# Weight conversion wholly through PSUM, block sums ranked last, and a last batch in two equal parts

## The chip, the cores and the metric

The kernel runs on one core of one Trainium2 chip. The metric is the device time of one execution in microseconds (us), as the median of several runs. One further execution is recorded by the hardware profiler; its rows are what this text reads.

## What is computed

```python
# B, H, S, D = 4, 8, 768, 64
k_sum = k.reshape(B, H, 24, 32, D).max(axis=3)
v_sum = v.reshape(B, H, 24, 32, D).mean(axis=3)
scores_l = where(|pos_q - pos_k| < 16, scale * q @ k.T, -1e9)
scores_s = scale * q @ k_sum.T + log(32)
a = softmax(concat([scores_l, scores_s]))
x = a @ concat([v, v_sum])            # -> [B, S, 512]
...
h = relu(x.T @ w_tok1) @ w_tok2       # 768 -> 256 -> 768 over tokens
u = x + h.T
out = u + relu(u @ w_ch1) @ w_ch2     # 512 -> 1536 -> 512 over channels
```

All in float32. The weights are doubles in memory and reach the core as such.

## The kernel before

**Stages.** Each batch goes through attention (local window of 96 keys and 24 block summaries for each tile of 64 queries, heads in four pairs p), the token mix (`t1`, then `up`), and the channel mix. The channel mix takes most of the time. It is done in two halves of the tokens, 512 and 256 (`HT`), and in 12 slices f of the inner 1536: `ch1` puts u @ w_ch1 of one slice in a PSUM tile `hp` (12 matmuls), ACT writes its relu rounded (L843) and DVE the remainder (L848) into `h`, and `ch2` adds h @ w_ch2 to four output tiles `acc` (12 matmuls, L874). A float32 product is three passes with a rounded part and a remainder of each operand (`w1h`, `w1l`, `w2h`, `w2l`). In a name such as hp_0_0_8 the numbers are batch, half and slice; in sc_8_0 and et_8_0, and in av_8, the first is batch times 8 plus head.

**What runs beside it.** While PE works through the channel mix of batch b, the attention of batch b+1 is put between the products: scores `sc` (24 matmuls), softmax on DVE and ACT (`e`, L440 and L450), transposes `et`, and `av`. For batch 1 this stands in the last slices of batch 0 and later. The softmax output x is put away to memory in the transposed layout (`xaway`) and fetched again as `xT` (`fetch_x`, L530), where DVE adds the token mix to it (L787) and ACT and POOL split the sum into u. The block sums of v are loaded separately (`vb`, L268), reduced by DVE into `vs` (L382, eight of 96x512 for batch 1), scaled by POOL (L390) and written behind v by a DMA (v<-vs, L295); `av` reads them.

**The weights** are converted on the chip, in 30 ticks of 128x512 values. Ticks 6 to 29 are the channel weights: tick 6+2f is w1 of slice f, tick 7+2f is w2 of it. A tick is a load of the 64-bit words (L1005, SP queue), |high word| on ACT (L1035), a clamp on POOL (L1039), three steps on DVE (shift L1044, sign L1051, low bits L1058), the rounded part on ACT (L1080) and the remainder on POOL (L1086). What the shift and the sign leave is kept in `between`:

```python
psum = 10 <= i < 24
...
if psum:
    pb = bank(f"wp_{i}", ["att"])
    between, bkey = (lambda: pb.t.bitcast(I32)), (pb, 0)
else:
    between, bkey = mid, parts[0]
```

so ticks 10 to 23 keep it in a PSUM bank of the tag `att` (two banks, which the attention's scores use too; name `wp`), the others in SBUF (name `wb`). Ticks run during batch 0's first half, a few slices ahead of their use.

**The order.** A planner (class `Plan`) simulates the engines with a cost for each step (`took`), gives each step a rank (`R_H`, `R_EVAC`, `R_ATT`, `R_LATER`, `R_W`, from 0 to 4, the lowest first) and writes out one fixed order for each engine. An engine then takes its instructions in that order and waits at the first that isn't ready. SP issues nearly all DMAs, in one queue.

Of the kernel before, what the change touches and what calls it, by code (L numbers as in the profile page):

```python
# [34 lines left out]
HT = (512, 256)  # L35
H0 = (0, 512)
# [150 lines left out]
def tile_attention_mixer(  # L187
# [438 lines left out]
    def turn_x(b, p):  # L626

        x2, a = x_t[b, p]
        e = sbuf([P, S], "e", f"xb_{b}_{p}", 3)
        add(  # L630
            "dve", 1.05,
            lambda: nc.vector.transpose(
                e.t.rearrange("p (t c) -> p t c", c=P), x2.t[:, :, a, :]
            ),
            reads=x_keys(b, p), writes=[(e, 0)], rank=R_ATT,
        )
        for half, nt in enumerate(HT):
            cs = slice(H0[half], H0[half] + nt)
            away = xa_t[b, half, p] = plan.slot(
                dram, [P, nt], F32, f"xaway{half}", f"xaway_{b}_{half}_{p}", 4  # L640
            )
            add(
                "sp", 0.4, lambda away=away, cs=cs: nc.sync.dma_start(out=away.t, in_=e.t[:, cs]),
                reads=[(e, 0)], writes=[(away, 0)], kb=nt // 2,
            )
# [103 lines left out]
    def tok2(b, half, p):  # L749
        (x2, a), t1 = x_t[b, p], t1_t[b, p]  # L750
        h0, nt = H0[half], HT[half]
# [4 lines left out]
        u = u_t[b, half, p] = sbuf([P, 2, nt], f"u{half}", f"u_{b}_{half}_{p}", 4, F32R)  # L756
# [25 lines left out]
        if far:  # L782
# [3 lines left out]
                "dve", 0.6 if half == 0 else 0.42,  # L786
# [6 lines left out]
                "act", 0.5 if half == 0 else 0.38,  # L793
# [13 lines left out]
            "act", 0.5 if half == 0 else 0.38,  # L807
# [4 lines left out]
            "dve", 0.6 if half == 0 else 0.42,  # L812
# [8 lines left out]
    def ch1(b, half, f):  # L821
        nt = HT[half]
        pt = mm_bank(f"hp_{b}_{half}_{f}")
        h = h_t[f] = sbuf([P, 2, nt], ("h", "ot")[half], f"h_{b}_{half}_{f}", 2, F32R)
# [3 lines left out]
        def products():  # L828
# [13 lines left out]
            "act", 0.5 if half == 0 else 0.36,  # L842
# [4 lines left out]
            "dve", 0.57 if half == 0 else 0.37,  # L847
# [10 lines left out]
    def ch2(b, half, f):  # L858
        h, nt = h_t.pop(f), HT[half]
# [128 lines left out]
    def w_tick(i, behind=()):  # L988
# [22 lines left out]
        psum = 10 <= i < 24  # L1011
# [57 lines left out]
        add("dve", 0.6 if psum else 0.5, shift, reads=parts, writes=[bkey], rank=rank)  # L1069
# [62 lines left out]
    start = [sum(HT[j // NF] // 256 for j in range(i)) for i in range(2 * NF + 1)]  # L1132
    for b in range(B):
# [126 lines left out]
```

## Time and profile before

| | us |
|---|---|
| median of three runs | 582.44 (581.02 to 582.76) |
| the profiled execution, device time | 582.82 |
| its span, first to last instruction | 581.0 |
| TensorE matmul (PE) busy | 564.6 (97%) |
| VectorE (DVE) busy | 288.3 (50%) |
| ScalarE (ACT) busy | 216.6 (37%) |
| GpSimd (POOL) busy | 153.5 (26%) |

An idle stretch of PE is where time can be had, as long as PE's work stays what it is. The time of an idle stretch is read from the rows in which PE waits, and what it waited for stands in brackets behind it.

### The profile page before, as it was taken

The numbers are of one execution on the slowest core, as the hardware profiler recorded it, in microseconds if no ns is written. First come the engines' busy times: TensorE is split into PE (matmuls) and PEld (weight loads), VectorE is DVE, ScalarE is ACT, GpSimd is POOL, SyncE is SP. The second block draws the span as 40 slices with busy tenths as digits, with TensorE's granted clock in tenths as the row PEclk, the third lists the DMA queues.
The fourth block names the chain that finished last, engine by engine and source line by source line (L and its number), as shares of the span: only waits on it lengthen the run. The fifth ranks groups of instructions, "written<-read, shape, count | busy, mean of one in ns | idle before, by whom it ended". The sixth has DMA issues, their size and how long they took to land.

```text
span 581.0 us, 12315 instructions
## 1 busy us (share of the span) xinstructions
PE 564.6 (97%) x4701; PEld 487.9 (84%) x4701; DVE 288.3 (50%) x872; ACT 216.6 (37%) x697; POOL 153.5 (26%) x191
## 2 busy tenths in 40 slices
PE   7889999989999999999999999999999998999997
PEld 3678888768989988878899988888899997888997
DVE  3698799996563255644733336442543321110311
ACT  4677665536564343222334224222434111110110
POOL 0236586744033310000085010000085021000500
PEclk9999999989999999999999999999999999999999
DMA  8854568643664027847775127745454012000101
GB/s 294 304 164 129 184 211 263 215 154 129 193 193 152 18 74 198 231 109 200 213 177 131 23 56 190 199 134 136 123 142 91 6 26 49 1 0 1 70 4 37
DMA packets 116778, 75.89 MB, mean 131 GB/s; under 512 B 86640, under 2 KB 99056, under 8 KB 116720
## 3 DMA queue, kind: packets, MB, share of 16 engines
q1 hardware_dynamic: 116720, 75.12, 45.8%
q8 instruction: 37, 0.61, 0.4%
q14 instruction: 21, 0.17, 0.1%
HBM read 57.59 MB, written 15.73 MB: 126 GB/s over the span
## 4 chain that ended last, share of the span: by engine, by line
PE 80%; DVE 11%; DMA 4%; ACT 2%; issue 2%; SPq 1%; POOL 1%; DVEq 0%; ACTq 0%
PE acc L874 30%; PE hp L831 29%; PE t1q L730 5%; PE up L770 4%; PE av L557 4%; PE sc L426 4%; DMA w<-in_w_ch 2%; DVE wb L1058 2%; PE warm L1099 1%; PE et L488 1%; DMA k<-in_kw 1%; DVE wb L1051 1%; DVE wp L1051 1%; DVE wp L1044 1%; DVE vs L382 1%
## 5 line engine op out<-in xcount | busy, mean ns | idle before, releaser
L874 PE MATMUL acc<-h,w2h 128*128 128x512 f32 (+1 forms) x768 | 205.0, 340 | 2.1 <-DVE h L848 2.1
L831 PE MATMUL hp<-u,w1h 128*128 128x512 f32 (+1 forms) x768 | 191.5, 339 | 0.0
L874 PEld LDWEIGHTS acc<-h,w2h 128*128 128x128 f32 x768 | 134.4, 189 | 20.6 <-DVE h L848 3.3
L831 PEld LDWEIGHTS hp<-u,w1h 128*128 128x128 f32 x768 | 131.2, 190 | 16.2 <-issue 1.3
L848 DVE SCALAR_TENSOR_TENSOR h<-hp,h 128x512 fp32r<-128x512 f32 (+1 forms) x96 | 53.2, 554 | 161.1 <-ACT h L843 161.0
L831 PE MATMUL hp<-u,w1l 128*128 128x256 f32 (+1 forms) x384 | 129.4, 337 | 0.3 <-POOL w1l L1086 0.3
L874 PE MATMUL acc<-h,w2l 128*128 128x256 f32 (+1 forms) x384 | 129.2, 336 | 0.0
L843 ACT ACTIVATE h<-hp 128x512 fp32r<-128x512 f32 (+1 forms) x96 | 46.9, 488 | 205.4 <-PE hp L831 204.3
L450 ACT ACTIVATE e<-e,den 128x120 f32<-128x120 f32 x192 | 73.3, 385 | 49.8 <-DVE den L440 49.7
L831 PEld LDWEIGHTS hp<-u,w1l 128*128 128x128 f32 x384 | 72.6, 189 | 8.4 <-POOL w1l L1086 0.7
L874 PEld LDWEIGHTS acc<-h,w2l 128*128 128x128 f32 x384 | 72.5, 189 | 6.9
L935 POOL TENSOR_TENSOR ot<-ot,u 128x512 f32<-128x512 f32 (+1 forms) x28 | 29.1, 1062 | 133.0 <-DVE ot L927 133.0
L440 DVE CUSTOM_DVE_ANT_0 e<-sc,mask_sb 128x120 f32<-128x120 f32 x192 | 41.4, 277 | 13.7 <-PE sc L426 12.4
L770 PE MATMUL up<-wt2h,t 128*128 128x256 f32 (+1 forms) x128 | 37.3, 350 | 1.6 <-DVE xT L787 1.6
L409 POOL MEMSET e<- 128x48 f32 x16 | 2.3, 141 | 131.1 <-DMA away<-e 68.6
L450 ACT ACTIVATION_READ_ACCUMULATOR e<-e,den 128x1 f32 x192 | 36.2, 189 | 0.0
L716 POOL TENSOR_TENSOR xs<-x,xs 128x512 fp32r<-128x512 f32 x18 | 23.5, 1306 | 28.1 <-ACT xs L711 28.1
L426 PE MATMUL sc<-k,q 64*64 64x120 f32 x768 | 28.6, 274 | 1.8 <-PE et L488 0.7
L426 PEld LDWEIGHTS sc<-k,q 64*64 64x64 f32 x768 | 20.9, 134 | 10.7 <-issue 6.8
L730 PE MATMUL t1q<-xs,ws 128*128 128x256 f32 x216 | 28.7, 284 | 0.0
L557 PEld LDWEIGHTS av<-v,eT 120*64 120x64 f32 x768 | 23.9, 138 | 4.8 <-issue 2.5
L730 PEld LDWEIGHTS t1q<-xs,ws 128*128 128x128 f32 x216 | 27.2, 191 | 0.4
(73 smaller groups left out, 595.0 us busy)
## 6 DMA issues: line engine op xcount, KB each, us to landing
w<-in_w_ch SPq DMA_DIRECT2D x48, 256.0 KB
k<-in_kw SPq DMA_DIRECT2D x16, 720.0 KB
v<-in_vw SPq DMA_DIRECT2D x32, 288.0 KB
q<-in_q SPq DMA_DIRECT2D x16, 384.0 KB
away<-e SPq DMA_DIRECT2D x16, 384.0 KB
eT<-away SPq DMA_DIRECT2D x64, 96.0 KB
out<-ot SPq DMA_DIRECT2D x16, 256.0 KB
w<-in_w_tok SPq DMA_DIRECT2D x12, 256.0 KB
```

The costliest lines, as they stand in the source:

```text
L426: nc.tensor.matmul(tiles[j].t[c * QT : (c + 1) * QT, i * NC : (i + 1) * NC], lhsT=qt.t[rows, t * QT : (t + 1) * QT], rhs=kt.t[rows, t, :], ...
L440: nc.vector.tensor_tensor_reduce(out=e.t[:, j, i * P : i * P + NC], in0=tiles[j].t[:, i * NC : (i + 1) * NC], in1=mask_sb[:, mv, :], op0=A ...
L450: nc.scalar.activation(ei, ei, AF.Exp, bias=den_t[n].t[:, 1, T : T + 1], scale=-1.0, accum_out=den_t[n].t[:, 0, T : T + 1],)
L557: nc.tensor.matmul(pv[cs, T], lhsT=eT[:NC, T % (TT // 2), cs], rhs=v.t[:NC, 2 * T + c], start=True, stop=True,)
L716: lambda slot=slot, src=src: nc.gpsimd.tensor_tensor(out=slot.t[:, 1], in0=src(), in1=slot.t[:, 0].bitcast(F32), op=ALU.subtract),
L730: nc.tensor.matmul(pt.t[:, 2 * P * k : 2 * P * (k + 1)], lhsT=ws[:, wp, T, ks], rhs=xs[:, xp, T], start=(c == 0 and k == 0 and T == 0 and ...
L770: nc.tensor.matmul(pt.t[:, :nt], lhsT=t1.t[:, part, ks], rhs=w[:, k, h0 : h0 + nt], start=(far and k == 0 and i == 0), stop=(k == DTOK // ...
L831: nc.tensor.matmul(pt.t[:, :nt], lhsT=w[:, c, fs], rhs=us[c].t[:, part], start=(i == 0), stop=(i == len(ops) - 1),)
L843: lambda: nc.scalar.activation(h.t[:, 0], pt.t[:, :nt], AF.Relu),
L848: lambda: nc.vector.scalar_tensor_tensor(out=h.t[:, 1], in0=pt.t[:, :nt], scalar=0.0, in1=h.t[:, 0].bitcast(F32), op0=ALU.max, op1=ALU.sub ...
L874: nc.tensor.matmul(slot.t[:, c0 : c0 + nt], lhsT=w[:, f, o * P : (o + 1) * P], rhs=h.t[:, part], start=(f == 0 and w is w2h and part == 0 ...
L935: lambda view=view, u=u: nc.gpsimd.tensor_tensor(out=view(), in0=view(), in1=u.t[:, 1].bitcast(F32), op=ALU.add),
```

## The change

1. All channel-weight ticks from 10 on keep `between` in PSUM, so ticks 24 to 29 too. The planner's costs of the DVE steps are set anew.
2. The eight block sums of v for batch 1 get rank `R_W + 1`, behind the weights, instead of `R_LATER`, before them.
3. The last batch is cut 384/384 instead of 512/256, and the planner's costs follow the width (`spent`). The put-away x goes in slots by width; u of its second half takes other tags; its `acc` tiles take a bank each in both halves; the outputs of its first half are kept in tag `k`.
4. `fetch_x` of the second half comes a slot earlier in the program, and the last two odd output DMAs go through ACT's queue.

```diff
-HT = (512, 256)
-H0 = (0, 512)
+HT = ((512, 256),) * (B - 1) + ((384, 384),)
+H0 = ((0, 512),) * (B - 1) + ((0, 384),)
...
-            reads=[(slot, 0)], writes=[(s, ("sum", c))], rank=R_LATER,
+            reads=[(slot, 0)], writes=[(s, ("sum", c))], rank=R_W + 1 if b == 1 else R_LATER,
...
-                dram, [P, nt], F32, f"xaway{half}", f"xaway_{b}_{half}_{p}", 4
+                dram, [P, nt], F32, f"xaway{nt}", f"xaway_{b}_{half}_{p}", 8
...
+    def spent(nt, quarter, half):
+
+        return quarter + (half - quarter) * (nt - 256) / 256
...
-        u = u_t[b, half, p] = sbuf([P, 2, nt], f"u{half}", f"u_{b}_{half}_{p}", 4, F32R)
+        tag, bufs = f"u{half}", 4
+        if b == B - 1 and half:
+            tag, bufs = (("e", 3), ("q", 2))[p // 2]
+        u = u_t[b, half, p] = sbuf([P, 2, nt], tag, f"u_{b}_{half}_{p}", bufs, F32R)
...
-        h = h_t[f] = sbuf([P, 2, nt], ("h", "ot")[half], f"h_{b}_{half}_{f}", 2, F32R)
+        h = h_t[f] = sbuf([P, 2, nt], "ot" if nt == 256 else "h", f"h_{b}_{half}_{f}", 2, F32R)
...
-                    slot = sbuf([P, n, nt], "h", f"ot_{b}_{half}_{o}", 2)
+                    slot = sbuf([P, n, nt], "k" if nt == 384 else "h", f"ot_{b}_{half}_{o}", 2)
...
-            add(
-                "sp", 0.06,
-                lambda view=view, o=o: nc.sync.dma_start(
+            eng, queue = ("act", nc.scalar) if o in ur_t and o % 2 else ("sp", nc.sync)
+            add(
+                eng, 0.06,
+                lambda view=view, o=o, queue=queue: queue.dma_start(
...
-        psum = 10 <= i < 24
+        psum = i >= 10
...
         stt = 0.7 if room else 0.85
+        if not psum and not first:
+            stt = 0.95 if room else 1.2
...
-        add("dve", 0.6 if psum else 0.5, shift, reads=parts, writes=[bkey], rank=rank)
+        add("dve", 0.69, shift, reads=parts, writes=[bkey], rank=rank)
...
+                if b >= FAR and u1s[p] == slot + 1:
+                    fetch_x(b, 1, p)
                 if u1s[p] == slot:
-                    if b >= FAR:
-                        fetch_x(b, 1, p)
                     tok2(b, 1, p)
```

How the order moves is shown at three places. The first is DVE in batch 0, where the weights of slice 9 (ticks 24 and 25) begin. Before, the last block sum stands between ticks 22 and 23, seven others stand further up, and tick 24 works in SBUF:

```order
L1058 SCALAR_TENSOR_TENSOR wb_22_1338<-w_22_1279,wp_22_1461 128x512
L382 TENSOR_REDUCE vs_1_1310<-vb_1_7_1451 96x16
L1044 TENSOR_SCALAR wp_23_1489<-wb_23_1365 128x512
L848 SCALAR_TENSOR_TENSOR h_0_0_7_1481<-hp_0_0_7_1438,h_0_0_7_1481 128x512
L1051 SCALAR_TENSOR_TENSOR wp_23_1489<-w_23_1303,wp_23_1489 128x512
L1058 SCALAR_TENSOR_TENSOR wb_23_1365<-w_23_1303,wp_23_1489 128x512
L1044 TENSOR_SCALAR wb_24_1402<-wb_24_1402 128x512
```

After, the same stretch of DVE's order:

```order
L1067 SCALAR_TENSOR_TENSOR wb_22_1340<-w_22_1279,wp_22_1417 128x512
L1053 TENSOR_SCALAR wp_23_1438<-wb_23_1369 128x512
L1060 SCALAR_TENSOR_TENSOR wp_23_1438<-w_23_1305,wp_23_1438 128x512
L1067 SCALAR_TENSOR_TENSOR wb_23_1369<-w_23_1305,wp_23_1438 128x512
L1053 TENSOR_SCALAR wp_24_1465<-wb_24_1399 128x512
L1060 SCALAR_TENSOR_TENSOR wp_24_1465<-w_24_1333,wp_24_1465 128x512
L1067 SCALAR_TENSOR_TENSOR wb_24_1399<-w_24_1333,wp_24_1465 128x512
L856 SCALAR_TENSOR_TENSOR h_0_0_7_1486<-hp_0_0_7_1440,h_0_0_7_1486 128x512
```

Tick 24 is done before the remainder of slice 7 (h_0_0_7), and no block sum stands there. They now follow the last weight step, among the work of slices 10 and 11; six stand ahead of the first softmax of batch 1 (e_4_0) and two behind it:

```order
L1067 SCALAR_TENSOR_TENSOR wb_29_1518<-w_29_1467,wp_29_1604 128x512
L384 TENSOR_REDUCE vs_1_1629<-vb_1_0_1263 96x16
L384 TENSOR_REDUCE vs_2_1633<-vb_2_0_1514 96x8
L384 TENSOR_REDUCE vs_1_1629<-vb_1_1_1265 96x16
L384 TENSOR_REDUCE vs_1_1629<-vb_1_2_1267 96x16
L856 SCALAR_TENSOR_TENSOR h_0_0_10_1655<-hp_0_0_10_1614,h_0_0_10_1655 128x512
L313 TENSOR_REDUCE ks_5_1676<-k_5_1572 128x24
L322 COPY k_5_1572<-ks_5_1676 128x12x24
L384 TENSOR_REDUCE vs_1_1629<-vb_1_3_1636 96x16
L384 TENSOR_REDUCE vs_2_1633<-vb_2_1_1639 96x8
L384 TENSOR_REDUCE vs_1_1629<-vb_1_4_1659 96x16
L856 SCALAR_TENSOR_TENSOR h_0_0_11_1706<-hp_0_0_11_1679,h_0_0_11_1706 128x512
```

The second place is PE in batch 0 at slice 8. Before, `hp` of slice 8 follows the twelve `acc` products of slice 7 and is followed by `hp` of slice 9:

```order
L874 MATMUL acc_0_0_3_1089<-h_0_0_7_1481,w2h_78 128x512
L831 MATMUL hp_0_0_8_1527<-u_0_0_0_886,w1h_76 128x512 x2
L831 MATMUL hp_0_0_8_1527<-u_0_0_0_886,w1l_77 128x512
L831 MATMUL hp_0_0_8_1527<-u_0_0_1_909,w1h_76 128x512 x2
L831 MATMUL hp_0_0_8_1527<-u_0_0_1_909,w1l_77 128x512
L831 MATMUL hp_0_0_8_1527<-u_0_0_2_934,w1h_76 128x512 x2
L831 MATMUL hp_0_0_8_1527<-u_0_0_2_934,w1l_77 128x512
L831 MATMUL hp_0_0_8_1527<-u_0_0_3_1014,w1h_76 128x512 x2
L831 MATMUL hp_0_0_8_1527<-u_0_0_3_1014,w1l_77 128x512
L831 MATMUL hp_0_0_9_1555<-u_0_0_0_886,w1h_76 128x512 x2
```

After, PE has `hp` of slice 8 ahead of the `acc` products of slice 7:

```order
L882 MATMUL acc_0_0_3_1092<-h_0_0_6_1424,w2h_78 128x512
L839 MATMUL hp_0_0_8_1501<-u_0_0_0_893,w1h_76 128x512 x2
L839 MATMUL hp_0_0_8_1501<-u_0_0_0_893,w1l_77 128x512
L839 MATMUL hp_0_0_8_1501<-u_0_0_1_913,w1h_76 128x512 x2
L839 MATMUL hp_0_0_8_1501<-u_0_0_1_913,w1l_77 128x512
L839 MATMUL hp_0_0_8_1501<-u_0_0_2_937,w1h_76 128x512 x2
L839 MATMUL hp_0_0_8_1501<-u_0_0_2_937,w1l_77 128x512
L839 MATMUL hp_0_0_8_1501<-u_0_0_3_1015,w1h_76 128x512 x2
L839 MATMUL hp_0_0_8_1501<-u_0_0_3_1015,w1l_77 128x512
L882 MATMUL acc_0_0_0_1089<-h_0_0_7_1486,w2h_78 128x512
```

So a product of twelve matmuls now stands between each `hp` and the `acc` that needs it. Behind this, slices 9 to 11 alternate in the same way, and the first scores of batch 1 (sc_8_0, sc_9_0) stand one product earlier.

The third place is PE at the start of the last batch, where the token mix of the second half (`up`, pairs 2 and 3) still has to be done. Before, the two stand in a row ahead of the first `acc`:

```order
L770 MATMUL up_3_1_2_5807<-wt2l_82,t1_3_2_5492 128x256
L770 MATMUL up_3_1_2_5807<-wt2h_81,t1_3_2_5492 128x256
L770 MATMUL up_3_1_3_5819<-wt2h_81,t1_3_3_5495 128x256
L770 MATMUL up_3_1_3_5819<-wt2l_82,t1_3_3_5495 128x256
L770 MATMUL up_3_1_3_5819<-wt2h_81,t1_3_3_5495 128x256 x2
L770 MATMUL up_3_1_3_5819<-wt2l_82,t1_3_3_5495 128x256
L770 MATMUL up_3_1_3_5819<-wt2h_81,t1_3_3_5495 128x256
L874 MATMUL acc_3_0_0_5829<-h_3_0_0_5794,w2h_78 128x512
```

After, the first `acc` product (twelve matmuls, the first three shown) stands between pair 2 and pair 3:

```order
L779 MATMUL up_3_1_2_5807<-wt2l_82,t1_3_2_5514 128x384
L779 MATMUL up_3_1_2_5807<-wt2h_81,t1_3_2_5514 128x384
L882 MATMUL acc_3_0_0_5817<-h_3_0_0_5798,w2h_78 128x384
L882 MATMUL acc_3_0_0_5817<-h_3_0_0_5798,w2l_79 128x384
L882 MATMUL acc_3_0_0_5817<-h_3_0_0_5798,w2h_78 128x384
```

## Rows read from the trace of the kernel before

**Rows 1.** The page, its first part: busy us, share and instructions of each engine.

```profile
PE 564.6 (97%) x4701; PEld 487.9 (84%) x4701; DVE 288.3 (50%) x872; ACT 216.6 (37%) x697; POOL 153.5 (26%) x191
```

**Rows 2.** Windows: stretch, length, busy of PE, PEld, DVE, ACT, POOL, PEclk, DMA, GB/s.

```profile
66.00:106.00 40.00, 40.00 (x178) 32.84 (x177) 36.05 (x65) 24.22 (x57) 28.22 (x42) 1.00 0.74 228
106.00:123.00 17.00, 14.61 (x55) 10.78 (x53) 16.76 (x26) 6.98 (x18) 13.41 (x16) 0.90 0.69 224
```

**Rows 3.** Waits of PE: who waited for whom, us in total, times, longest.

```profile
PE et L488 <- DVE x L569: 0.8, 1, 0.8
```

**Rows 4.** Timeline of PE, 106 to 123: start, us, instruction [idle before <- releaser].

```profile
106.90 0.39 PE L874 MATMUL acc<-h,w2l 128*128 128x512 f32 x1
107.61 0.74 PE L874 MATMUL acc<-h,w2h 128*128 128x512 f32 x2 [0.32 <-DVE h L848]
...
112.77 0.61 PE L831 MATMUL hp<-u,w1h 128*128 128x512 f32 x2
113.66 0.50 PE L831 MATMUL hp<-u,w1l 128*128 128x512 f32 x1 [0.27 <-POOL w1l L1086]
...
116.36 0.39 PE L874 MATMUL acc<-h,w2l 128*128 128x512 f32 x1
118.55 0.73 PE L874 MATMUL acc<-h,w2h 128*128 128x512 f32 x2 [1.80 <-DVE h L848]
...
122.44 0.72 PE L831 MATMUL hp<-u,w1h 128*128 128x512 f32 x2
```

**Rows 5.** Timeline of DVE: two ticks in PSUM form, then the late ones in SBUF.

```profile
75.23 0.69 DVE L1044 TENSOR_SCALAR wp<-wb 128x512 int32<-128x512 int32 x1
...
77.29 0.69 DVE L1044 TENSOR_SCALAR wp<-wb 128x512 int32<-128x512 int32 x1
...
105.69 0.68 DVE L382 TENSOR_REDUCE vs<-vb 96x16 f32<-96x512 f32 x1
...
108.80 0.42 DVE L1044 TENSOR_SCALAR wb<-wb 128x512 int32<-128x512 int32 x1
...
111.02 0.96 DVE L1044 TENSOR_SCALAR wb<-wb 128x512 int32<-128x512 int32 x1
...
114.07 0.97 DVE L1044 TENSOR_SCALAR wb<-wb 128x512 int32<-128x512 int32 x1
```

**Rows 6.** Groups of DVE by form: count | busy us, mean ns | idle before.

```profile
L382 DVE TENSOR_REDUCE vs<-vb 96x16 f32<-96x512 f32 x8 | 5.1, 673 | 0.0
```

**Rows 7.** Timeline of POOL: the same remainder step beside PSUM and SBUF ticks.

```profile
106.83 1.44 POOL L1086 TENSOR_TENSOR w1l<-wb,w1h 128x256 fp32r<-128x256 f32 x2
...
112.42 2.33 POOL L1086 TENSOR_TENSOR w1l<-wb,w1h 128x256 fp32r<-128x256 f32 x2
```

**Rows 8.** Timeline of ACT: the longest wait for a weight's load.

```profile
92.69 0.66 ACT L1035 ACTIVATE wb<-w 128x512 f32<-128x512 f32 x1 [1.82 <-DMA w<-in_w_ch]
```

**Rows 9.** Timeline of PE, later: the first scores of batch 1.

```profile
128.09 0.85 PE L426 MATMUL sc<-k,q 64*64 64x120 f32 x24
```

**Rows 10.** Timeline of DVE at 170: the block maximum ahead of x.

```profile
170.22 0.95 DVE L311 TENSOR_REDUCE ks<-k 128x24 f32<-128x768 f32 x1 [2.10 <-DMA k<-in_kw]
```

**Rows 11.** Timeline of PE and DVE at the start of the last batch.

```profile
473.82 0.63 PE L831 MATMUL hp<-u,w1h 128*128 128x512 f32 x2
...
481.33 0.42 DVE L787 TENSOR_TENSOR xT<-up,xT 128x256 f32<-128x256 f32 x1 [2.62 <-DMA xT<-xaway]
...
481.81 0.39 PE L770 MATMUL up<-wt2h,t 128*128 128x256 f32 x1 [1.64 <-DVE xT L787]
```

**Rows 12.** The chain that ended last: twelve matmuls of 512 and of 256 columns.

```profile
510.00 2.72 PE acc L874 x12
...
569.83 1.45 PE hp L831 x12
```

**Rows 13.** Timeline of DVE and SP at the end.

```profile
576.37 1.46 DVE L927 TENSOR_TENSOR ur<-acc,ur 128x256 f32<-128x256 f32 x4 [1.35 <-PE acc L874]
...
576.82 1.79 SPq L942 DMA_DIRECT2D out<-ur  x4
```

More of the change, by code (lines that the diff above doesn't have):

```diff
@@ L636, in turn_x @@
         )
-        for half, nt in enumerate(HT):
-            cs = slice(H0[half], H0[half] + nt)
+        for half, nt in enumerate(HT[b]):
+            cs = slice(H0[b][half], H0[b][half] + nt)
             away = xa_t[b, half, p] = plan.slot(
-                dram, [P, nt], F32, f"xaway{half}", f"xaway_{b}_{half}_{p}", 4
+                dram, [P, nt], F32, f"xaway{nt}", f"xaway_{b}_{half}_{p}", 8
             )
@@ L774, in products @@
                     )
-        took = (1.45, 0.75) if far else (2.0, 1.1)
         add(
-            "pe", took[half], products,
+            "pe", spent(nt, 0.75, 1.45) if far else spent(nt, 1.1, 2.0), products,
             reads=([] if far else x_keys(b, p)) + [(t1, 0), (t1, 1)] + [("wt2", i) for i in range(3)],
@@ L785, in tok2 @@
             add(
-                "dve", 0.6 if half == 0 else 0.42,
+                "dve", spent(nt, 0.42, 0.6),
                 lambda: nc.vector.tensor_tensor(
@@ L792, in tok2 @@
             add(
-                "act", 0.5 if half == 0 else 0.38,
+                "act", spent(nt, 0.38, 0.5),
                 lambda: nc.scalar.activation(u.t[:, 0], xT.t, AF.Copy),
@@ L806, in tok2 @@
         add(
-            "act", 0.5 if half == 0 else 0.38,
+            "act", spent(nt, 0.38, 0.5),
             lambda: nc.scalar.activation(u.t[:, 0], pt.t[:, :nt], AF.Copy),
@@ L811, in tok2 @@
         add(
-            "dve", 0.6 if half == 0 else 0.42,
+            "dve", spent(nt, 0.42, 0.6),
             lambda: nc.vector.tensor_tensor(
@@ L841, in ch1 @@
         add(
-            "act", 0.5 if half == 0 else 0.36,
+            "act", spent(nt, 0.36, 0.5),
             lambda: nc.scalar.activation(h.t[:, 0], pt.t[:, :nt], AF.Relu),
@@ L846, in ch1 @@
         add(
-            "dve", 0.57 if half == 0 else 0.37,
+            "dve", spent(nt, 0.37, 0.57),
             lambda: nc.vector.scalar_tensor_tensor(
@@ L858, in ch2 @@
     def ch2(b, half, f):
-        h, nt = h_t.pop(f), HT[half]
+        h, nt = h_t.pop(f), HT[b][half]
         n = 512 // nt
@@ L896, in residual @@
     def residual(b, half, o):
-        u = u_t[b, half, o]
-        slot = ur_t[o] = sbuf([P, 2 * HT[0]], "u0", f"ur_{o}", 4)
+        u, nt = u_t[b, half, o], HT[b][half]
+        slot = ur_t[o] = sbuf([P, nt], "u0", f"ur_{o}", 4)
         add(
-            "pool", 0.7,
+            "pool", spent(nt, 0.7, 1.2),
             lambda: nc.gpsimd.tensor_tensor(
-                out=slot.t[:, : HT[half]], in0=u.t[:, 0].bitcast(F32),
+                out=slot.t, in0=u.t[:, 0].bitcast(F32),
                 in1=u.t[:, 1].bitcast(F32), op=ALU.add,
@@ L909, in finish @@
     def finish(b, half):
-        h0, nt = H0[half], HT[half]
-        n = 2 * HT[0] // nt
+        h0, nt = H0[b][half], HT[b][half]
+        n = 1024 // nt
         for o in range(NC4):
             u, (bank_o, c0) = u_t.pop((b, half, o)), acc[o]
-            took = 0.57 if half == 0 else 0.37
+            took = spent(nt, 0.37, 0.57)
             if o in ur_t:
                 slot = ur_t[o]
-                view = lambda slot=slot: slot.t[:, :nt]
+                view = lambda slot=slot: slot.t
                 key, other, more = (slot, 0), view, [(slot, 0)]
@@ L933, in finish @@
                 add(
-                    "pool", 1.2 if half == 0 else 0.7,
+                    "pool", spent(nt, 0.7, 1.2),
                     lambda view=view, u=u: nc.gpsimd.tensor_tensor(
@@ L1128, in tile_attention_mixer @@
     tok2(0, 0, NP - 1)
-    start = [sum(HT[j // NF] // 256 for j in range(i)) for i in range(2 * NF + 1)]
+    start = [sum(HT[0][j // NF] // 256 for j in range(i)) for i in range(2 * NF + 1)]
     for b in range(B):
```

12 lines of the change are left out of this document (6 added, 6 removed).

## The prediction

> **What bounds the kernel now.** I read the page first: PE is busy for 97% of the span [rows 1], so a change can only win where PE stands still, runs slowly, or is left waiting at either end. The windows, the list of PE's waits and its timeline then say where that is. From 66 to 106 PE has no gap, while DVE is busy for 36.05 of 40 us. From 106 to 123 PE is busy for only 14.61 of 17 us at a mean clock of 0.90, and DVE for 16.76 of 17 [rows 2]. That is the stage of the late weights: DVE is what is late, and PE pays. The timeline of PE gives the price [rows 4]. Twelve 512-column matmuls take 2.72 us when nothing disturbs them, 0.227 each [rows 12]. The matmul at 106.90 is followed after 0.71 (0.48 too much, waiting for the remainder of h), the pair at 112.77 after 0.89 (0.44 too much, for POOL's remainder of w1), the one at 116.36 after 2.19 (1.96 too much, for h again). Together 2.9 us. Behind the last one PE needs 3.89 us, from 118.55 to 122.44, for ten matmuls that are worth 2.27: the clock fell to the lower level after the long wait, and that costs another 1.6. So this stage loses **4.5 us**.
>
> Elsewhere there is little: 0.8 where `et` waits for x at about 172 [rows 3], 1.64 at the start of the last batch [rows 11], and the tail, in which the last evacuations start at 576.37 and the last output is issued at about 578.6 [rows 13] while the span ends at 581.0. The sum is made against the profiled execution's own 582.82, which lies 0.38 above the median of 582.44.
>
> **Part 1, the block sums.** Eight reduces of 96x512 cost DVE 5.1 us [rows 6], all before the late weights; the last ends just after 106 [rows 5]. Behind the weights they cost the same, but the first eleven slices no longer wait for them. So tick 24, which DVE begins at 108.80 [rows 5], can begin some 5 us earlier. What could take DVE's place as the late one is the load: the longest wait of ACT for a weight is 1.82 at 92.69 [rows 8]. It eats at most that much of the 5 us, and three block-sum loads of 192 KB also leave the queue's stretch there.
>
> **Part 2, PSUM for ticks 24 to 29.** A tick in PSUM form takes 2.06 (75.23 to 77.29). In SBUF form tick 24 takes 2.22 and tick 25 3.05 [rows 5], the latter while POOL works. POOL suffers too: the same remainder step takes 1.44 beside PSUM ticks and 2.33 beside SBUF ones [rows 7]. I take a gain of 2 us on DVE over the six ticks (bounds: a loss of about 2, when POOL is idle and the shift's 0.69 instead of 0.42 [rows 5] counts in full, and a gain of 6, at 1 us a tick). None of this is on the path by itself: it adds to the 5 us.
>
> The shift shows 0.42 with both sides in SBUF and 0.69 with PSUM. The Trainium skill ("VectorE: DVE Perf Modes", section "Why PSUM operands drop a tier") says that a PSUM operand rules out the mode that needs both SBUF read ports, which speaks against this part: by that page alone the six ticks would cost DVE 6 x 0.27 = 1.6 more. Its page "SBUF — State Buffer", section "Who interferes with whom", says that a DVE instruction with two SBUF inputs contends with a GpSimd one that reads SBUF, and one with a single SBUF input doesn't; that speaks for it, and the slow rows on both engines agree. I count the stretch by the rows.
>
> **Sum of the stage.** With 5 + 2 us in hand, w1 of slice 8 is ready at about 104 instead of 108.3 (the remainder step at 106.83 [rows 7]), so PE can take `hp` of slice 8 at 106.9, right behind `acc` of slice 6, as the order of after has it. Its remainder h would be ready at about 112.3; `acc` of slice 8 comes up at about 106.9 + 3 x 2.72 = 115.1. Before, h was late by 2; now it is early by almost 3. All three waits go, and with them the half-speed stretch, since nothing else stops PE there: **-4.5**. What is late next are the two PSUM banks. The first scores of batch 1 (sc_8_0) come one product earlier and reuse banks that ticks 28 and 29 now hold until about 120.6, while PE gets there at about 120.2: **+0.4** (0 to 1.5). Queued behind that wait on PE are `acc` of slice 9 and all that follows, so every tenth of it counts.
>
> On DVE the block sums now stand among slices 10 and 11 and ahead of the first softmax. Six of them, 4 us, delay e_4_0 to about 129 to 130; the second scores, which need its bank back, come up at about 131: hidden, with under 1 us to spare. v of batch 1 is complete once POOL has scaled vs and the DMA has landed, by my count at about 135; `av` of batch 1 comes at about 144: hidden by 9 us. On SP the block-sum loads moved behind w_29, and k and q of batch 1 with them; the scores of batch 1 stood at 128.09 before [rows 9] and their loads still come first among those moved: nothing.
>
> **Part 3, 384/384.** No row has 384 columns. Twelve matmuls take 2.72 at 512 and 1.45 at 256 [rows 12], so on a straight line 2.09 at 384, and two halves of 384 cost what one of 512 and one of 256 cost: **0**. The far bounds are the rates of the two neighbours, 0.121 and 0.227 a matmul against my 0.173, which over 576 matmuls would be about -30 and +31 us; I take the line between them, since the two rows make a step of 0.015 plus 0.00041 a column, so that nearly all of a matmul is its columns, and keep +-1 us. At the half boundary four `acc` banks must be evacuated instead of reused in pairs, four steps of under 0.69 beside two `hp` products of 2.1 each: hidden.
>
> At the **start of the last batch** PE waits 1.64, 1.92 from start to start less the matmul's own 0.12 = 1.8 in all [rows 11]: `up` of pair 3 needs the bank that DVE frees by adding xT, and xT came late from memory (2.62). In the new order the first `acc` product of 2.1 us lies between pair 2 and pair 3, and the fetch is issued a slot earlier, but `up` of pair 2 comes one wait forward. From the spacing of SP's issues I get waits of about 0.35 and 0.6: **-0.85** (0 to -1.8).
>
> The **tail**: the last `acc` is four groups of three matmuls of 384, with one evacuation of about 0.55 behind the last (0.36 a piece for 256 columns by [rows 13]), and the four output issues (0.45 each on one queue, [rows 13]) go over two queues. Against that, 768 KB instead of 512 KB have to land. **-0.3** (+0.3 to -0.6). Here the Trainium skill ("DMA: Bandwidth & Descriptors", section "Issuing engines are not separate DMA queues") warns that a second issuing engine saves only the issuing time; by it alone the longer transfer would make the tail 0 to +0.3. No row separates the two.
>
> **The rest**: x at 172 waits for ks, which waited 2.10 for its load [rows 10]; a vb load ahead of it has moved, so some 0.6 earlier: **-0.3** (0 to -0.8). In the first 60 us a few steps change places (vm of pair 3 ahead of `av`), for which I see no reason either way: 0 (+-0.8). At the end of batch 0 `up` of pair 3 comes closer to the first `hp` that needs it: **+0.1** (0 to 0.3). Batches 1 and 2 keep PE's order.
>
> Sum: -4.5 + 0.4 - 0.85 - 0.3 - 0.3 + 0.1 = -5.45 against 582.82, so 577.4; on the scale of the median **577.0**.
>
> **The rivals.**
> A, the forecast: the stage of the late weights closes up. 577.0, with its own range of 574.8 to 579.5.
> B, the wait only moves: the banks of ticks 28 and 29, or the six block sums ahead of e_4_0, stop PE at the first or second scores. Margins of +0.4 and under 1 us are thin, and DVE is full until 130. If it happens for about as long as the wait removed, PE also loses its clock again: 577.0 - 0.4 + 1.96 + 1.6 = 580.2.
> C, the change doesn't do what it says: the weights were held back by their loads, not by DVE (the 1.82 in [rows 8] and a DMA share of 0.74 speak for it; DVE's 36.05 of 40 against [rows 2]), so slice 8's weights come no sooner and the 4.5 us stay, now as a wait at the earlier `hp`. Only the rest remains: 582.44 - 0.85 - 0.3 - 0.3 = 581.0.
> D, slower: v of batch 1 is late. The last two block sums stand behind e_4_0's softmax, then come POOL's scaling and a DMA in SP's one queue, behind k and q. `av` of batch 1 needs it at about 144, and each us beyond that is a us of PE. From 147.5 on the gain over the range of equal times is gone, from 151 on the kernel is slower by over 0.3%; a landing at 153 gives 577.0 + 9 = 586. My count of 135 speaks against, the long queue on SP for it.
>
> **How the numbers follow.** A 0.60, B 0.20, C 0.11, D 0.09. The prediction is A's 577.0. A measurement of this kernel tells 0.3%, 1.75 us, from no change: faster is below 580.7, slower above 584.2. A gives all of its chance to faster, B about three quarters; C lies within; D is mostly slower: faster 0.75, same 0.16, slower 0.09. The range of 574.5 to 581.5 takes in A, B and most of C; it leaves out D and about as much in the outer parts of the others.
>
> **What would show it.** Right: between 106 and 123 PE has no wait over 0.3 for h or w1l and its clock stays at the upper level; L1058 of ticks 24 to 29 shows 0.7 and POOL's L1086 about 1.4; `sc` at about 120 waits for under 1 us. B: PE waits for L1058 or L440 between 119 and 133. C: ACT's waits for loads between 90 and 105 grow to over 4 us. D: `av` of batch 1 waits for a DMA. The part on 384 is wrong if a product of twelve takes other than 2.05 to 2.13; the start of the last batch is right if its two waits sum to under 1.2.

## The result

The changed kernel takes 578.18 us (median of 14 runs, 574.71 to 580.4) where the kernel before takes 582.75 (14 runs as well). The ratio is 0.990 (0.9876 to 0.9925), so 4.4 to 7.2 us less. 577.0 (574.5 to 581.5) was forecast.

The profiled execution took 574.71, with a span of 572.9 against 581.0. That pair overstates the difference: its first scores came at 7.28 instead of 8.47, because the warm-up ran at the higher clock earlier (its matmuls start 0.43 us apart until 4.2 us into the span here and until 6.6 in the trace before, and 0.22 apart behind that). That is no work of the change: no_actq, which has the same start, came to them at 8.29 (more on it at the end). I therefore read the difference by stretches that hold the same work in every kernel:

| stretch | before | after | |
|---|---|---|---|
| up to the first scores | 8.47 | 7.28 | -1.19 |
| from there to the first channel product of batch 0 | 57.16 | 57.62 | +0.46 |
| **batch 0**: from there to the first product of batch 1 | 141.70 | 135.09 | **-6.61** |
| batches 1 to 3, to the end of the last matmul | 369.63 | 369.25 | -0.39 |
| tail, to the end of the span | 4.07 | 3.68 | -0.39 |

Batch 0 is read between the first `hp` products of batch 0 and of batch 1, before and then after:

```profile
65.63 0.63 PE L831 MATMUL hp<-u,w1h 128*128 128x512 f32 x2
...
207.33 0.63 PE L831 MATMUL hp<-u,w1h 128*128 128x512 f32 x2
```

```profile
64.90 0.63 PE L839 MATMUL hp<-u,w1h 128*128 128x512 f32 x2
...
199.99 0.63 PE L839 MATMUL hp<-u,w1h 128*128 128x512 f32 x2
```

The page and the windows of the stage, after; the rows of before are [rows 1] and [rows 2], and the columns are the same:

```profile
PE 560.2 (98%) x4701; PEld 497.8 (87%) x4701; DVE 283.0 (49%) x872; ACT 215.6 (38%) x697; POOL 152.4 (27%) x191
```

```profile
66.00:106.00 40.00, 40.00 (x178) 33.10 (x178) 36.06 (x63) 26.28 (x62) 31.11 (x47) 1.00 0.72 225
106.00:123.00 17.00, 17.00 (x96) 13.80 (x95) 16.62 (x32) 5.92 (x14) 9.04 (x13) 1.00 0.62 210
```

PE is busy without a gap from 106 to 123 at the full clock, where it had 14.61 of 17 us at 0.90. DVE is as full as before; it is only further ahead. PE's timeline, where [rows 4] showed three waits, has none; the products of slices 7 to 10 and the first scores follow each other directly:

```profile
105.72 0.61 PE L839 MATMUL hp<-u,w1h 128*128 128x512 f32 x2
...
108.44 0.39 PE L882 MATMUL acc<-h,w2h 128*128 128x512 f32 x1
...
111.17 0.61 PE L839 MATMUL hp<-u,w1h 128*128 128x512 f32 x2
...
113.89 0.39 PE L882 MATMUL acc<-h,w2h 128*128 128x512 f32 x1
...
116.61 0.61 PE L839 MATMUL hp<-u,w1h 128*128 128x512 f32 x2
...
119.42 0.84 PE L428 MATMUL sc<-k,q 64*64 64x120 f32 x23
```

On DVE the remainder of h for slice 7 and the one for slice 8 are there 3 us before `acc` asks for them at 108.44 and 113.89, the copy of k that the first scores need is done at 117.5, and the last weight step at 118.1:

```profile
104.59 0.68 DVE L856 SCALAR_TENSOR_TENSOR h<-hp,h 128x512 fp32r<-128x512 f32 x1
...
110.15 0.68 DVE L856 SCALAR_TENSOR_TENSOR h<-hp,h 128x512 fp32r<-128x512 f32 x1
...
117.16 0.31 DVE L322 COPY k<-ks 128x288 f32<-128x288 f32 x1
117.39 0.68 DVE L1067 SCALAR_TENSOR_TENSOR wb<-w,wp 128x512 int32<-128x512 int32 x1
117.99 2.19 DVE L384 TENSOR_REDUCE vs<-vb 96x16 f32<-96x512 f32 x4
```

### The profile page after: what moved, and what is told of

It is laid out like the page before. It is cut to its first block, busy times and chain, and to the rows that moved or that the text cites. A ratio compares the mean times of both kernels' runs of the same rounds, so it can differ in the third digit from the quotient of the medians.

```text
span 572.9 us, 12330 instructions
## 1 busy us (share of the span) xinstructions
PE 560.2 (98%) x4701; PEld 497.8 (87%) x4701; DVE 283.0 (49%) x872; ACT 215.6 (38%) x697; POOL 152.4 (27%) x191
## 4 chain that ended last, share of the span: by engine, by line
PE 90%; DVE 4%; ACT 3%; POOL 1%; issue 1%; SPq 1%; DMA 0%; DVEq 0%
PE hp L839 35%; PE acc L882 35%; PE t1q L736 5%; PE up L779 5%; PE sc L428 4%; PE av L559 4%; ACT e L452 2%; PE et L490 1%; PE warm L1110 1%; ACT eT L501 1%; PE up L771 1%; PE t1p L689 0%; DVE wb L1060 0%; ACT wb L1044 0%; DMA xT<-xaway 0%
## 5 line engine op out<-in xcount | busy, mean ns | idle before, releaser
L882 PE MATMUL acc<-h,w2h 128*128 128x512 f32 (+2 forms) x768 | 205.8, 338 | 0.0
L839 PE MATMUL hp<-u,w1h 128*128 128x512 f32 (+2 forms) x768 | 192.7, 338 | 0.0
L839 PEld LDWEIGHTS hp<-u,w1h 128*128 128x128 f32 x768 | 132.7, 189 | 12.6 <-issue 1.4
L856 DVE SCALAR_TENSOR_TENSOR h<-hp,h 128x512 fp32r<-128x512 f32 (+2 forms) x96 | 53.0, 552 | 154.5 <-ACT h L851 154.4
L839 PE MATMUL hp<-u,w1l 128*128 128x512 f32 (+2 forms) x384 | 128.9, 336 | 0.0
L882 PE MATMUL acc<-h,w2l 128*128 128x512 f32 (+2 forms) x384 | 128.4, 334 | 0.0
L851 ACT ACTIVATE h<-hp 128x512 fp32r<-128x512 f32 (+2 forms) x96 | 46.9, 489 | 201.5 <-PE hp L839 200.2
L943 POOL TENSOR_TENSOR ot<-ot,u 128x512 f32<-128x512 f32 (+2 forms) x28 | 27.9, 1018 | 108.8 <-DVE ot L935 107.4
L779 PE MATMUL up<-wt2h,t 128*128 128x256 f32 (+2 forms) x128 | 37.7, 352 | 1.1 <-DVE xT L795 0.7
```

The costliest lines, as they stand in the source:

```text
L779: nc.tensor.matmul(pt.t[:, :nt], lhsT=t1.t[:, part, ks], rhs=w[:, k, h0 : h0 + nt], start=(far and k == 0 and i == 0), stop=(k == DTOK // ...
L839: nc.tensor.matmul(pt.t[:, :nt], lhsT=w[:, c, fs], rhs=us[c].t[:, part], start=(i == 0), stop=(i == len(ops) - 1),)
L851: lambda: nc.scalar.activation(h.t[:, 0], pt.t[:, :nt], AF.Relu),
L856: lambda: nc.vector.scalar_tensor_tensor(out=h.t[:, 1], in0=pt.t[:, :nt], scalar=0.0, in1=h.t[:, 0].bitcast(F32), op0=ALU.max, op1=ALU.sub ...
L882: nc.tensor.matmul(slot.t[:, c0 : c0 + nt], lhsT=w[:, f, o * P : (o + 1) * P], rhs=h.t[:, part], start=(f == 0 and w is w2h and part == 0 ...
L943: lambda view=view, u=u: nc.gpsimd.tensor_tensor(out=view(), in0=view(), in1=u.t[:, 1].bitcast(F32), op=ALU.add),
```

## The experiments

All times are medians, with the kernel before run beside them (583.2 to 583.9). "Batch 0" is the stretch of the table above, in the profiled execution. It is the same work in all of these kernels (late_dve adds to it).

**The three edits that touch the weight stage.** They are the rank of the block sums, the PSUM form of ticks 24 to 29, and the planner's costs of the DVE steps. First each was taken out of the changed kernel.

no_rank, the sums ahead of the weights again:

```diff
-rank=R_W + 1 if b == 1 else R_LATER
+rank=R_LATER
```

> The changed kernel, with the block sums of batch 1 ranked ahead of the weights again (5.1 us of DVE). Theory DVE-late (the gain comes from taking those sums out of DVE's way): the wait for h before the acc of slice 8 is back, less what PSUM ticks save, 1 to 3 us in all and the lower clock behind it, so about 581 (580 to 582.5). Theory PSUM (the gain comes from the PSUM form of ticks 24 to 29, the sums were covered anyway): no wait over 0.5, 578 to 579. Theory loads (weights wait for their DMAs): the same wait of PE in this kernel and in the changed one, 578 to 579, with ACT waiting for loads just as long.

Measured: 578.85, ratio 0.9918 (0.9892 to 0.9944); batch 0 137.18. In the weight stage PE waits 0.34 once, at the scores. Most of the gain stays without the rank.

no_psum, ticks 24 to 29 in SBUF:

```diff
-psum = i >= 10
+psum = 10 <= i < 24
```

> The changed kernel, with ticks 24 to 29 in SBUF form again. Theory DVE-late: the sums' 5 us cover the 2 us or so that the SBUF form costs, no wait of PE over 0.5 between 100 and 125, 578 to 579. Theory PSUM: the waits are back, 581 to 583. Either way the steps L1067 of these ticks take 0.9 to 1.1 where POOL works and POOL's remainder 1.8 to 2.3, against 0.7 and 1.4 to 1.6.

Measured: 578.19, ratio 0.9899 (0.9863 to 0.9934); batch 0 135.03. Nothing is lost, though the steps are as slow as foretold: 1.12 for L1067 where POOL works.

Then the rank alone, on the kernel before (only_rank):

```diff
-rank=R_LATER
+rank=R_W + 1 if b == 1 else R_LATER
```

> The kernel before, with only the rank of the eight block sums changed. Theory DVE-late: it takes nearly the whole gain of the weight stage, 4 to 5 us, so 578 to 579 against 582.6. Theory PSUM: it takes 1 to 2, and waits of over 1 us for h stay between 105 and 125, 581 to 582.

Measured: 584.38, ratio 1.0022 (0.9996 to 1.0047); batch 0 142.29. Neither theory foresaw this: the part that I had credited with 5 us brings nothing alone. DVE does get its 5 us: tick 25 begins at 105.66 instead of 111.02 [rows 5]. But PE's order was the new one, and its waits were elsewhere. DVE, and then PE, of this kernel:

```profile
105.66 0.96 DVE L1044 TENSOR_SCALAR wb<-wb 128x512 int32<-128x512 int32 x1
...
119.96 1.12 DVE L1058 SCALAR_TENSOR_TENSOR wb<-w,wb 128x512 int32<-128x512 int32 x1
121.00 1.00 DVE L382 TENSOR_REDUCE vs<-vb 96x16 f32<-96x512 f32 x2
121.93 0.67 DVE L848 SCALAR_TENSOR_TENSOR h<-hp,h 128x512 fp32r<-128x512 f32 x1
122.52 1.26 DVE L382 TENSOR_REDUCE vs<-vb 96x16 f32<-96x512 f32 x2
123.71 0.94 DVE L311 TENSOR_REDUCE ks<-k 128x24 f32<-128x768 f32 x1
124.68 0.31 DVE L320 COPY k<-ks 128x288 f32<-128x288 f32 x1
```

```profile
116.43 0.73 PE L874 MATMUL acc<-h,w2h 128*128 128x512 f32 x2 [1.13 <-DVE h L848]
125.09 0.85 PE L426 MATMUL sc<-k,q 64*64 64x120 f32 x24 [3.38 <-issue]
```

```profile
123.00:131.00 8.00, 5.91 (x39) 4.72 (x40) 5.23 (x10) 0.00 (x0) 0.06 (x1) 0.79 0.46 141
```

PE stands 3.4 us ahead of the first scores and starts them when the copy of k is done, then runs at a mean clock of 0.79 (column before DMA). In DVE's fixed order that copy stood behind all weights and four block sums (three of batch 1 and a smaller one of batch 2). The planner believed the SBUF ticks to take 1.9 us (0.5 + 0.7 + 0.7; 2.2 for ticks 26 and 27), while those from 24 on took 2.3 to 3.7; so it expected a DVE with time to spare, and on the chip DVE came there late. The place is that of the forecast's rival B, the first scores, though PE waits there for the copy of k and not for a bank. That led to a new theory, "cost": what counts is that the planner's times are those of the chip. Four kernels test it.

only_psum, on the kernel before:

```diff
-psum = 10 <= i < 24
+psum = i >= 10
```

> The kernel before, with ticks 24 to 29 in PSUM form and nothing else. Theory DVE-late: the sums' 5 us are still in the way and PSUM gives back 2 to 4 on DVE and POOL, so a wait of about 1 for h or the scores stays: 579.5 to 582 against 583. Theory cost (what counts is that the times that the planner assumes for ticks 24 to 29 are those that they take; in PSUM form they are): no wait over 0.7 between 105 and 130, 578.5 to 580.

Measured: 579.23, ratio 0.9934 (0.9909 to 0.9958); batch 0 137.55; the longest wait of PE that the timeline names in the stage is 0.35, for h. With the SBUF ticks turned into PSUM ones, the old costs are near what the steps take.

no_both, the changed kernel without rank and without PSUM:

```diff
-rank=R_W + 1 if b == 1 else R_LATER
+rank=R_LATER
...
-psum = i >= 10
+psum = 10 <= i < 24
```

> The changed kernel, with the block sums ahead of the weights and ticks 24 to 29 in SBUF form: what is left is the planner's new costs and the last batch. Theory cost: the planner now knows that these ticks are slow and puts the scores and the products where the weights really are, so that over half of the stage's gain stays: 579 to 580.5. Theory DVE-late: the weights come as late as before, PE waits 2 to 4 us between 105 and 130, 581.5 to 583.

Measured: 579.9, ratio 0.9941 (0.9915 to 0.9967); batch 0 138.34. DVE does the same work as before in the stage, in the same form, and about half of the gain is there: the order alone, built on truer times, is worth 3.4 us. What stays in the stage is one wait for POOL's remainder:

```profile
114.13 0.50 PE L839 MATMUL hp<-u,w1l 128*128 128x512 f32 x1 [0.97 <-POOL w1l L1097]
```

rank_cost, the kernel before with rank and costs:

```diff
-rank=R_LATER
+rank=R_W + 1 if b == 1 else R_LATER
...
+        if not psum and not first:
+            stt = 0.95 if room else 1.2
...
-add("dve", 0.6 if psum else 0.5, shift, ...)
+add("dve", 0.69, shift, ...)
```

> The kernel before, with the rank of the block sums and the planner's new costs (0.95 and 1.2 for the SBUF form, 0.69 for the shift), ticks 24 to 29 still in SBUF. Theory cost: the 3.5 us that PE waited at the first scores when the rank alone was changed are gone (there the block maximum of k stood behind the last weights and three sums on DVE; now it stands ahead of the last two ticks), 578.5 to 580. Theory PSUM-needed (the rank can't win without PSUM): a wait of 2 to 4 at the scores stays, 582 to 584.

Measured: 578.87, ratio 0.9928 (0.9902 to 0.9954); batch 0 136.13. No wait of PE between 100 and 131. The first scores stand one product later (123.04), and DVE has the maximum of k ahead of the last step of tick 28 and of tick 29. (In batch 0 all engines have the order of no_psum, so the edits of the last batch change nothing there.) DVE's rows:

```profile
118.17 0.94 DVE L311 TENSOR_REDUCE ks<-k 128x24 f32<-128x768 f32 x1
119.14 0.31 DVE L320 COPY k<-ks 128x288 f32<-128x288 f32 x1
119.37 0.69 DVE L1058 SCALAR_TENSOR_TENSOR wb<-w,wb 128x512 int32<-128x512 int32 x1
```

old_cost, the changed kernel with the old costs (the last two edits of rank_cost undone):

> The changed kernel with the costs of before for the three DVE steps of a tick (0.6, 0.7, 0.85). Its order puts four block sums ahead of the block maximum of k that the first scores need. Theory cost: with all these ticks in PSUM the old costs are nearly right, so nothing is lost, 578 to 579; PE waits under 0.7 at the scores. Rival: the place of that maximum decides whatever the form, a wait of 1 to 3 at the scores, 579.5 to 582.

Measured: 577.16, ratio 0.9905 (0.988 to 0.993); batch 0 136.48, with 0.62 from start to start at the first scores. As the cost theory has it: with every tick in PSUM the old numbers are nearly right. PE's order in batch 0 is the one of only_rank and of the changed kernel; so the 5.8 us between only_rank and old_cost are not PE's order but what PE waits for. The copy of k is done 59.3 us behind the first product of batch 0 in only_rank and 55.2 in old_cost:

```profile
122.98 0.31 DVE L322 COPY k<-ks 128x288 f32<-128x288 f32 x1
```

All eight combinations together, batch 0 in us:

| rank | PSUM | new costs | batch 0 |
|---|---|---|---|
| | | | 141.70 |
| x | | | 142.29 |
| | x | | 137.55 |
| | | x | 138.34 |
| x | x | | 136.48 |
| x | | x | 136.13, 135.03 |
| | x | x | 137.18 |
| x | x | x | 135.09, 135.48, 135.72, 136.06, 136.39 |

Where a combination was profiled more than once, all values stand (those of the last row are the changed kernel, no_384, spread, no_actq and better, which have one order in batch 0). They lie up to 1.3 apart, so less than that is not read. Nearly all of it stands behind the weight stage: all five reach the first product of the second half 63.6 to 63.8 us after the first of batch 0. PSUM alone brings 4.2 of the 6.6 and the costs alone 3.4; the rank brings nothing without one of them, 2.2 to 3.3 with the costs, and 1.1 with PSUM and 0.8 to 2.1 on top of both, which is hardly more than the spread.

**Is DVE's lateness a cause at all, or only the order?** late_dve leaves every engine's order as it is in the changed kernel and puts eight reductions that nobody reads ahead of tick 24, unknown to the planner:

```diff
 def shift():
+    for _ in range(8 if late else 0):
+        nc.vector.tensor_reduce(out=late.t, in_=mid().bitcast(F32), axis=AX, op=ALU.max)
     nc.vector.tensor_scalar(
```

> The changed kernel with eight more reductions of 128x512 (about 5.3 us of DVE) ahead of tick 24's shift, of which the planner knows nothing, so that every engine's order stays what it is. It puts DVE's lateness back without the order of before. In the changed kernel the first scores need the block maximum of k, which is there about 1.7 us before PE comes, and h of slices 7 and 8 about 3 us before. Theory DVE-late: PE waits about 3.6 us in all, at w1 of slice 9 or at the scores, and runs at the lower clock behind it: the stretch from the first product of batch 0 to the first of batch 1 goes from 135.1 to 138.5 to 141, the time to 581 to 584. Theory order (the order alone brought the gain, whatever DVE does): under 136.5, and 578 to 579.5.

Measured: 582.69, ratio 0.9984 (0.9958 to 1.0011); batch 0 140.89, +5.8 of the 6.6: by the medians the whole gain is gone. DVE and PE:

```profile
103.90 5.72 DVE L1056 TENSOR_REDUCE late<-wb 128x1 f32<-128x512 f32 x8
```

```profile
112.34 0.73 PE L882 MATMUL acc<-h,w2h 128*128 128x512 f32 x2 [1.74 <-DVE h L856]
124.58 0.39 PE L428 MATMUL sc<-k,q 64*64 64x120 f32 x2 [1.40 <-issue]
```

So lateness costs, when the order doesn't know of it: 5.7 us on DVE became 5.8 on PE, through 4.0 of waits from start to start and slow matmuls behind them. The same DVE work as before under an order that knows of it (no_both) costs 2.0 to 3.3 more than the changed kernel's order.

**The last batch.** no_384 cuts it 512/256 again:

```diff
-HT = ((512, 256),) * (B - 1) + ((384, 384),)
+HT = ((512, 256),) * B
...
-        if b == B - 1 and half:
-            tag, bufs = (("e", 3), ("q", 2))[p // 2]
```

> The changed kernel, with the last batch cut 512/256 again (its evacuations, slots and queues follow the width as the code has it). By the sum of the prediction: 0.85 at the start of the last batch and 0.3 of the tail are lost, 579.3 (578.7 to 580). Rival: the cut moves nothing, 578.2, its waits only shift. Rival: the halves of 384 cost more than they give, below 577.8.

Measured: 578.66, ratio 0.9924 (0.9892 to 0.9955); batches 1 to 3 369.53, tail 3.77. The cut moves 0.3 to 0.4 us in the trace, where the forecast gives it 0.85 + 0.3, and less than the medians can tell. Its rows say why it is so little. The wait at the start of the last batch is back, 1.59 from start to start against 1.04 in the changed kernel, but the products of the last batch cost 0.3 less (see 384 columns below):

```profile
477.36 0.38 PE L777 MATMUL up<-wt2h,t 128*128 128x256 f32 x1 [1.43 <-DVE xT L793]
```

no_actq issues all outputs on SP's queue:

```diff
-eng, queue = ("act", nc.scalar) if o in ur_t and o % 2 else ("sp", nc.sync)
+eng, queue = ("sp", nc.sync)
```

> The changed kernel with all output issues on SP's queue again. The stretch from the end of the last matmul to the end of the span is 3.68 us in the changed kernel, 4.07 in the one before, and 3.77 with the 512/256 cut and both queues. If the second queue is what shortened the tail: 4.0 to 4.2. If the four groups of three matmuls did: 3.6 to 3.8. The page of the skill on issuing engines allows the first as long as issuing is what the tail waits for.

Measured: 576.77 in one run; tail 3.64. The second queue gives nothing here. SP's row:

```profile
570.49 1.90 SPq L951 DMA_DIRECT2D out<-ur  x4
```

Four issues now come 0.52 apart, as the evacuations do, so that one queue keeps up; with the 256-column pieces of before they were ready 0.36 apart and went 0.45 apart [rows 13], which is where the second queue saves its 0.3 (no_384).

**A version beyond both.** better shortens the warm-up and spreads the token mix of the last batch's second half:

```diff
-for _ in range(21):
+for _ in range(13):
...
-u1s = (2, 3, 4, 5)
+u1s = (3, 5, 7, 9) if last else (2, 3, 4, 5)
...
-writes=[(pt, 0)], rank=R_ATT,
+writes=[(pt, 0)], rank=R_W if b == B - 1 and half else R_ATT,
```

> The changed kernel with two more edits. 13 instead of 21 warm-up matmuls: the first scores are ready at about 6.3 (copy of k), PE came to them at 7.28 to 8.68 by the clock that the warm-up had, so 1.0 to 2.0 earlier; if the fewer matmuls leave the clock low, that is lost again in the first 60 us. And the token mix of the last batch's second half spread over its slices 3 to 9 instead of at its start, where PE waits 0.45 and 0.59: 1.0 less. Together 2 to 3 us under the changed kernel, about 575.5 (574.5 to 577); if the clock suffers, 577 to 579.

Measured: 576.96, ratio 0.9873 (0.9835 to 0.991). Batches 1 to 3 took 368.07, 1.2 less than in the changed kernel: both waits are gone. The first scores came at 6.80, but the start behind them took 60.41. spread holds the second and third edit only:

> The changed kernel with only the second of the two edits of the run before: the token mix of the last batch's second half spread over its slices, and the warm-up of 21 matmuls as it was. In the run before, the two waits at the start of the last batch were gone and everything behind the first product of batch 1 took 1.16 less; the first scores came at 6.80, but the start behind them took 60.4 instead of 57.6. If the short warm-up gave nothing on balance: 577 (576.2 to 577.8), with the start behind the first scores at 57.6 where the clock holds. If the short warm-up was worth its 0.5 to 1.9: 577.5 to 578.5. If it did harm: below 576.3.

Measured: 577.62, ratio 0.988 (0.9836 to 0.9923), batches 1 to 3 368.31. The two lie within each other's intervals: what the short warm-up is worth stays open. The spread's 1 us is seen in both traces; the medians of both are below the changed kernel's 578.18, by less than the intervals can tell.

## Why the prediction held, point by point

**The stage closed up, as said.** All three waits and the half-speed stretch are gone. From the first product of batch 0 to `hp` of slice 10 it is 51.7 us instead of 56.8: -5.1 against the -4.5 forecast. The +0.4 at the scores did not come: I had the last ticks done at 120.6, and they were done at 118.1, before PE came at 119.4. Nor did the +0.1 at the end of batch 0: PE has no wait in this batch at all.

**The wait of `et` at 172** [rows 3] is 0.9 to 1.0 of the other 1.5 of batch 0, and part of that is luck. It is gone in the profiled execution, where I took 0.3 of it. But of the five executions that have the changed kernel's order in batch 0, it is gone in two and stays in three, with 0.42, 0.46 and 0.80; in no_actq it is as long as before. It goes with the wait of `ks`, which stands ahead of x in DVE's order, for its load of k: 1.17 and 1.40 where PE has no wait, 1.70, 1.78 and 2.10 in the other three. The rows of the changed kernel, then of no_actq:

```profile
166.87 0.95 DVE L313 TENSOR_REDUCE ks<-k 128x24 f32<-128x768 f32 x1 [1.17 <-DMA k<-in_kw]
```

```profile
168.88 0.95 DVE L313 TENSOR_REDUCE ks<-k 128x24 f32<-128x768 f32 x1 [2.10 <-DMA k<-in_kw]
...
171.35 1.01 PE L490 MATMUL et<-identf,e 128*120 128x128 f32 x6 [0.80 <-DVE x L571]
```

What the change itself gives at this place stays open; batch 0's safe gain is the 5.1 of the stage and little more.

**Whose gain it is was wrong.** The step "Part 1" credits the rank with 5 us of DVE time and "Part 2" calls PSUM an addition of 2. The 5 us of DVE time come with the rank alone, but the kernel's time does not move, since PE's wait moves to the first scores; PSUM alone brings 4.2, and the third edit, the planner's costs, worth 3.4 alone, stands in no line of my sum. I had treated the order of after as given and counted DVE's time under it. That gives the right end for the whole change and the wrong one for any part of it, because each part makes another order. The sizes of Part 2 were right: the DVE steps of ticks 24 to 29 take 13.0 us in all instead of 15.6, where a gain of 2 was forecast; L1067 takes 0.68 to 0.75 instead of up to 1.12. POOL's remainder beside them (compare [rows 7]):

```profile
112.62 1.45 POOL L1097 TENSOR_TENSOR w2l<-wb,w2h 128x256 fp32r<-128x256 f32 x2 [1.33 <-ACT w2h L1091]
115.06 1.45 POOL L1097 TENSOR_TENSOR w1l<-wb,w1h 128x256 fp32r<-128x256 f32 x2 [1.00 <-ACT w1h L1091]
```

The Trainium skill's rule on shared read ports ("SBUF — State Buffer", section "Who interferes with whom") agrees with this: 1.44 or 1.45 throughout, where the SBUF form had up to 2.33. The forecast told that rule too widely: the Trainium skill excepts the DVE instructions in modes that use both ports, and the shift, with its one SBUF input, takes 0.42 at best in SBUF but 0.96 and 0.97 in the two ticks that run beside POOL [rows 5]. The rule of the Trainium skill on PSUM operands ("VectorE: DVE Perf Modes", section "Why PSUM operands drop a tier") holds for the shift (0.69 in PSUM form), but it was outweighed.

**384 columns** cost nearly what the line said. The chain, after, gives 2.09 and 2.08 for twelve matmuls where 2.09 was forecast:

```profile
558.82 2.09 PE hp L839 x12
560.90 2.08 PE acc L882 x12
```

Over the 576 matmuls of these products in the last batch that is 0.3 more than before (99.95 against 99.67 us, from the starts in the timeline, waits left out), where the sum has 0.

**The start of the last batch**: waits of 0.45 and 0.59 from start to start, where 0.35 and 0.6 were forecast, against 1.8: -0.77 instead of -0.85. In the other kernels with the 384/384 cut and the token mix at its old place the two waits sum to 0.7 to 1.4, so the size varies. PE's rows:

```profile
470.39 0.44 PE L779 MATMUL up<-wt2h,t 128*128 128x384 f32 x1 [0.29 <-DVE xT L795]
...
474.23 0.44 PE L779 MATMUL up<-wt2h,t 128*128 128x384 f32 x1 [0.42 <-DVE xT L795]
```

**The tail** is -0.39 where -0.3 was forecast, by another cause. I counted on the two queues; the widths alone do it (no_actq). What the Trainium skill says of a second issuing engine ("DMA: Bandwidth & Descriptors", section "Issuing engines are not separate DMA queues") is what one sees: the queue saved issuing time, and only where issuing was late.

**v of batch 1** (rival D): its DMAs were issued from 131.8 to 133.7, and `av` came at 143.15 without a wait; forecast were v complete at 135 and `av` at 144. Rival C is out, since no wait for a load took the place of the old ones (ACT's longest for one between 80 and 121 is 0.88, where it was 1.82). Rival B did not happen in the changed kernel, but waits at the first scores are what only_rank and late_dve show, and both take longer than the 580.2 that B was priced at.

**The start**, put at 0, costs about 0.4: in the profiles whose clock stays at the upper level from 17 us on, the stretch behind the first scores takes 57.2 with the order of before (two profiles) and 57.5 to 57.8 with that of after (seven).

**The sum.** Without the warm-up's luck the two traces differ by 6.9 us against 5.45 forecast, and by about 5.9 without the wait of `et`, which came back in other executions; the timed ratio says 4.4 to 7.2. That the total comes so close is in part luck: the stage gave more than its term and the scores cost nothing, while the start and the 384 columns cost what the sum has at 0.

## What to carry to other kernels

In a kernel whose order is fixed by a planner, a step that takes longer than the planner thinks can be paid twice: by its time, and by everything that was put behind it in the belief that it would be done. Making the model true, or the step as quick as the model, can be worth as much as taking work away. And an engine with time to spare in the mean can still stand at one place in its order: ask what stands behind the late step, not how busy the engine is. To tell order from work, add work that the planner doesn't know of, or give the planner the truth and leave the work.

## What the runs showed of the hardware that was not expected

The same start runs at different granted clocks from one execution to the next. Windows of the first stretch, of the changed kernel and of spread, which has the same instructions in the same order up to there (the clock is the column before DMA; 1.00 is the upper level, 2.4 GHz, and a mean below it has stretches at the lower one, 1.2 GHz):

```profile
8.00:45.00 37.00, 31.16 (x613) 26.11 (x602) 28.87 (x140) 29.15 (x119) 10.94 (x15) 1.00 0.80 253
```

```profile
8.00:45.00 37.00, 32.94 (x538) 27.94 (x532) 25.75 (x125) 25.15 (x104) 7.67 (x10) 0.82 0.75 241
```

With it, the start behind the first scores takes 57.6 in the one and 61.4 us in the other. When the clock falls matters more than whether it does. A fall between 12 and 14 us alone costs this stretch nothing: the changed kernel's start takes 57.5 and 57.6 in the two profiles without it and 57.5 to 57.8 in the five that have it. The five profiles in which the clock falls between 26 and 30 us (no_384, only_psum, better, old_cost and spread) take 59.1 to 61.4. Over the 14 runs of the changed kernel, those at a mean clock of 1.000 took 574.71 and 575.73, those at 0.988 579.16 and 580.4: 3.4 to 5.7 us between executions of one kernel that go with the clock, about as much as the change is worth. Whether a wait lowered the clock or the clock lengthened the run, these times alone don't tell. Two profiles of one kernel can therefore not be subtracted as a whole; stretches with the same work at the same clock can. What decides whether the clock holds in the start stays open.
